# Last batch of a fused attention and expert kernel: q and k banked by token range, x in halves, last stores over two queues

## The chip, the cores and the metric

The kernel runs on one core of a Trainium2 chip. The metric is the device time of one execution in microseconds (us); the time of the kernel before is the median of six executions. Work is spread over TensorE (PE, with its weight loads as PEld), VectorE (DVE), ScalarE (ACT), GpSimd (POOL) and SyncE (SP), which here only issues DMA transfers. Each engine takes its instructions in the order in which the kernel writes them.

## The reference

Two layers follow one another. The first is attention over 8 batches, 12 heads, 448 tokens and head size 64, with a soft cap on the scores:

```python
scores = cap * np.tanh(scale * (q @ k.T) / cap)
attn = softmax(scores)          # over the keys
x[b] = concat_heads(attn @ v)   # 448 x 768
```

The second takes `x` through four single-head causal attention experts and adds those of the two best gate values per token:

```python
w = softmax(top2(x @ w_gate))
for e in range(4):
    q, k, v = x @ wq[e], x @ wk[e], x @ wv[e]
    ye = softmax(causal(scale * q @ k.T)) @ v @ wo[e]
    out += (token picked e) * w * ye
```

## The kernel before, in words

**Body.** The first layer runs over 48 pairs of heads, six pairs per batch. For each pair PE fills score banks (`fill`, L459), ACT takes `tanh` out of them (`tanh`, L478, instruction at L483) and then one `exp` over the whole pair (`expo`, L488, instruction at L491). PE multiplies with v (`blk`, L509), DVE normalises (L528, L532), PE transposes the result and one copy puts it into `xT[b][:, j, :]` (`a_xt_tr`, `a_xt_out`), the slice j of x for that batch. The second layer of batch b is done while the pairs of batch b+1 run. The order on ACT is a fixed list, `prog`. What PE and DVE do between the fills is chosen by `Plan`, which keeps estimated clocks for PE, DVE and ACT. `do_fill` (L945) sets `rel`, the time at which ACT gives a score bank back, `cost`, PE's time for the fill, and lets `plan.pump` place other work ahead of the fill as long as that ends before ACT is due, less `cost` and a margin of 0.3.

**Tail.** The last batch (b = 7) has no following pairs to hide behind. `last_batch` (L1053) collects all that is left of batch 6 (called c), the last pairs' attention and the whole second layer of batch 7 as operations with estimated costs, engines, dependencies and PSUM banks; `Graph.solve` (L155) tries 4000 priority lists and keeps the order with the smallest estimated end. An operation that may run on either DVE or ACT (`both`, L1082) is given to the one that would end it first. Priorities are the length of the path to the end plus a hand-set bias (L1089 to L1099): operations of the first token half (A, tokens below `CUT` = 256) get +6, the output projections (`wo`) and stores of batch c get -`BW` = -4.

For batch 7 the tail holds, in the order of the data: pv of the last pair in two halves of tokens (`("pv", u, i)`); four transposes into one bank and one copy of 448 columns to `xT` (`("xtp", u)`, `("xt", u)`); q and k of two expert pairs r = 0, 1 in four banks of 448 columns each (`qk_mm`, L1045, six matmuls per bank, L670), each evacuated by one copy of 448 columns (`q_out`, `k_out`); gate logits in the spare columns of the bank of q, r = 1 (`logits`, L1183); v (`v_mm`, L1194); scores in banks A, B and C (`fill`, L1259; A is tokens below 256, B and C the rest), their `exp` (L1293), pv (`pv_mm`, L1320), normalisation and gate weight (L1340 to L1357), transposes (`ot_tr`, L1359), projection (`project`, L1152, matmuls at L809), copies to the output tile `ob` (`b_wo_out`, L817) and stores (`b_store`, L826, on the SP queue). A store waits for both column halves of its `ob` tile, except for the last window (n = 3, 64 rows), which is stored in two halves. Some of the q and k matmuls of the last batch (`EARLY`, L1051) are given to `Plan` and run before the tail.

Of the kernel before, what the change touches and what calls it, by code (L numbers as in the profile page):

```python
# [132 lines left out]
class Graph:  # L133
# [55 lines left out]
    def order(self, users, deps, count, prio, eps):  # L189
        n = len(self.ops)  # L190
        free = dict(self.free)
        left = [len(d) for d in deps]
        start_at = [o[6] for o in self.ops]
        pools = {k: list(v) for k, v in self.pools.items()}
        slot = dict(self.held)
        count = dict(count)
        ends = {}
        ready = [i for i in range(n) if not left[i]]
        out = []
        span = 0.0  # L200
        while ready:
            cand = []
            for i in ready:
                _, eng, _, _, groups, opens, _, _ = self.ops[i]
                t = start_at[i]
                pool = None
                if opens:
                    m = len(groups)
                    ts = [
                        (max(f for _, f in pools[k][0:m]), k) for k in opens if len(pools[k]) >= m  # L210
                    ]
                    if not ts:
                        continue
                    f, pool = min(ts)
                    t = max(t, f)
                e = min(eng, key=lambda e: max(t, free[e]) + eng[e])
                cand.append((max(t, free[e]), i, e, pool))
            if not cand:
                return None
            first = min(c[0] for c in cand)  # L220
            t, i, e, pool = max((c for c in cand if c[0] <= first + eps), key=lambda c: prio[c[1]])
            _, eng, _, _, groups, opens, _, _ = self.ops[i]
            end = t + eng[e]
            free[e] = end
            span = max(span, end + self.LAND * (e == "DMA"))
            ready.remove(i)
            out.append((t, len(out), i, e, pool))
            for g in groups:
                if opens:
                    slot[g] = pool  # L230
                    pools[pool].pop(0)
                ends[g] = max(ends.get(g, (t, 0.0)), (t, end + self.LAT[e]))
                count[g] -= 1
                if not count[g]:
                    insort(pools[slot[g]], ends[g])
            for u in users[i]:
# [9 lines left out]
def kernel(  # L246
# [576 lines left out]
        ps = s.pop(("wo", n, f))  # L823
        evac(ob[lo:128, f * (D // 2) : (f + 1) * (D // 2)], ps[lo:128, :], act)

    def b_store(b, n, fs=(0, 1)):  # L826
        lo = 64 if n == 3 else 0
        w = WIN[n]
        c = slice(fs[0] * (D // 2), (fs[-1] + 1) * (D // 2))
        nc.sync.dma_start(out[b, w + lo : w + 128, c], st[b]["ob", n][lo:128, c])  # L830

    def b_wo(b, n, f):
        b_wo_ps(b, n, f)
# [111 lines left out]
    def do_fill():  # L945
        nonlocal nfill
        o = reads[nfill]
        rel = ends[nfill - 2] if nfill >= 2 else 0.0
        cost = 0.42 if o[0] == "X" or o[2] else 0.19
        for d in fill_dep(o):  # L950
            plan.force(d)
        cost = plan.pe_time(cost, plan.pe)
        at = plan.act + sum(dur(x) for x in prog[pos : where[nfill]])
        plan.pump(rel, at - cost - 0.3)
        plan.pe = max(plan.pe, rel, *(plan.done[d] for d in fill_dep(o))) + cost
        fill(*o[1:]) if o[0] == "T" else b_fill(*o[1:])
        plan.done[("f", nfill)] = plan.pe + plan.LAT
        nfill += 1
# [10 lines left out]
    def slot(p):  # L969
# [25 lines left out]
        if p >= HP and p % HP == 0 and p < NP:  # L995
            batch(p // HP - 1)
        if p == NP - 2:
            for r, w in EARLY:
                for j in range(4):
                    g = ("qk", r, w)  # L1000
                    d = [("xt", NP - HP + j)] + [(*g, j - 1)] * (j > 0)
                    plan.add(
                        (*g, j), 0.19, 0.0, d, nom["E", NP - 1, 0] + j, qk_mm, r, w, j,
                        aux="open" if j == 0 else None, group=g,
                    )

# [33 lines left out]
    BANKS["C", 0] = [(r, k, max(k, KM * (k == TAIL)), S) for r in range(2) for k in (TAIL, 256)], 64  # L1040


    qk = {}

    def qk_mm(r, w, j):  # L1045
        if j == 0:
            qk[r, w] = bank([128, 512], f32, f"{w}ps_{B - 1}_{r}")
        b_qk_mm(B - 1, r, w, qk[r, w][:, 0:S], j, j + 1)


    EARLY = ((0, "q"), (0, "k"))  # L1051

    def last_batch():  # L1053

# [20 lines left out]
            dict(aux=[(0.0, t) for t in plan.aux], tail=[(0.0, t3)] * 4),  # L1075
        )

        BR, BA, BW, BX = 2.0, 6.0, 4.0, 4.0

        BOTH = ("aux", "tail")  # L1080

# [3 lines left out]
        def op(key, eng, deps, fn, *args, group=None, groups=(), opens=None):  # L1085
# [2 lines left out]
            f = (lambda e: fn(*args, e == "ACT")) if len(eng) > 1 else (lambda e: fn(*args))  # L1088
            bias = 0.0  # L1089
            if key[0] == "qk":  # L1090
                bias = BR * (key[1] == 0)
# [8 lines left out]
            G.op(key, eng, deps, f, groups, opens, after, bias)  # L1100


        for u in (p - 1, p):
            for i in range(2):
# [10 lines left out]
                op((*g, "rc"), {"DVE": 0.18}, [(*g, 1, 1)], a_pv_rc, u, i, group=g)  # L1115
                op((*g, "xk"), {"DVE": 0.43}, [(*g, "rc")], a_pv_xk, u, i, group=g)
            g = ("xtp", u)
            for i in range(2):
# [45 lines left out]
            op((*g, 2), both(0.57, 0.49), [(*g, rs[-1])], b_wo_out, b, n, f, group=g)  # L1164

        def store(b, n):
            for fs in ((0,), (1,)) if (b, n) == (B - 1, 3) else ((0, 1),):
                kb = max(0.62, 0.5 * len(fs) * (0.5 if n == 3 else 1.0))
                op(
                    ("st", b, n, fs), {"DMA": kb}, [("wo", b, n, f, 2) for f in fs], b_store, b, n,  # L1170
                    fs,
                )

        for n in range(4):
# [5 lines left out]
                store(c, n)  # L1180


        def logits(j):  # L1183
            for n in range(4):
                nc.tensor.matmul(
                    qk[1, "q"][:, S + E * n : S + E * (n + 1)],
                    xT[b][:, j, WIN[n] : WIN[n] + 128], wvg[:, j, E * Dh : E * Dh + E],
                    start=False, stop=(j == NDC - 1), skip_group_check=True,
                )
# [17 lines left out]

        def lg_out():
            nc.vector.tensor_copy(
                s["lg"], qk[1, "q"][:, S : S + 4 * E].rearrange("p (n e) -> p n e", e=E)  # L1210
            )

        def q_out(r, act=False):
            b_q_out(b, r, qk[r, "q"][:, 0:S], act)

        def k_out(r, act=False):
            b_k_out(b, r, qk[r, "k"][:, 0:S], act)

        x0 = p - NDC + 1
        for r in range(2):  # L1220
            for w in "qk":
                g = ("qk", r, w)
                for j in range(NDC):
                    if (*g, j) in plan.done:
                        G.held[g] = "aux"
                        continue
                    d = [("xt", x0 + j)] + [(*g, j - 1)] * (j > 0)
                    op(
                        (*g, j), {"PE": 0.19}, d, qk_mm, r, w, j, group=g,
                        opens=None if j else BOTH,  # L1230
                    )
                d = [(*g, NDC - 1)] + [("el", NDC - 1)] * (r == 1 and w == "q")
                op((*g, "out"), both(0.6, 0.53), d, q_out if w == "q" else k_out, r, group=g)
        g = ("qk", 1, "q")
        for j in range(NDC):
            d = [("xt", x0 + j), (*g, 0)] + [("el", j - 1)] * (j > 0)
# [4 lines left out]
        for m in range(2):  # L1241
            g = ("vl", m)
            prev = None
            for j0, j1 in ((0, 3), (3, 5), (5, 6)):
                for i in range(2):
                    d = [("xt", x0 + j1 - 1), prev or ("xtp", p, 0)]
# [9 lines left out]

        sl = {}

        def fill(x):  # L1259
            blocks, _ = BANKS[x]  # L1260
            for e in range(2):
# [2 lines left out]
            for i, (r, k0, q0, q1) in enumerate(blocks):  # L1264
                for e in range(2):
                    h = slice(64 * e, 64 * (e + 1))
                    nc.tensor.matmul(
                        sl[x, e][:, o : o + q1 - q0], s["ke", r][h, k0 : k0 + 128],
                        s["qe", r][h, q0:q1], start=(i == 0),
                        stop=(i == len(blocks) - 1 and x[0] == "B"), skip_group_check=True,  # L1270
                    )
                o += q1 - q0
# [24 lines left out]
        for x, (blocks, o0) in BANKS.items():  # L1297
            rs = {a[0] for a in blocks}
            for e in range(2):
# [8 lines left out]
            g = [("sL", x, e) for e in range(2)]  # L1308
            op(
                ("sL", x, "mm"), {"PE": dict(A=0.6, B=0.25, C=0.8)[x[0]]},  # L1310
                [("qk", r, w, "out") for r in rs for w in "qk"], fill, x, groups=g, opens=BOTH,
            )
            for e in range(2):
                op(
# [166 lines left out]
```

## Time and profile before

| What | Value |
|---|---|
| Median of 6 executions | 326.96 us (326.5 to 327.65) |
| The profiled execution, its own time | 326.9 us |
| Span of its instructions | 325.2 us |
| ACT busy | 307.2 us, 94% of the span |
| PE busy | 277.6 us, 85% |
| DVE busy | 215.0 us, 66% |
| POOL busy | 155.7 us, 48% |
| Mean granted TensorE clock | 0.981 |

Times below are microseconds from the first instruction of the profiled execution. In the views of the profile a row names the line of the kernel, the engine, the operation, what it writes and reads, the shape and how often it ran; a bracket at the end says how long the engine had been idle and what released it. A row of a table by stretches gives the busy time of each engine in the stretch. The time of an execution is 1.7 us more than its span (326.9 against 325.2); a change of the span is taken to be a change of the time.

### The profile page before, as it was taken

To read this page: it belongs to the slowest core of one execution; us is meant where nothing else is said; L and a number is where in the kernel's file an instruction comes from. 1 tells how busy PE (TensorE), PEld (TensorE's weight loads), DVE (VectorE), ACT (ScalarE), POOL (GpSimd) and SP (SyncE) were. 2 spreads that over 40 slices of the span, in tenths; PEclk is the share of its full clock that TensorE was granted. 3 is DMA by queue.
4 is the path that set the end of the run, shared out by engine and by line. 5 is a ranking of instruction groups with operands and counts; after the bars stand their busy time and mean duration, and the time that the engine had idled before them with its cause. 6 is when DMAs were issued, how large, how long until landed. Compare 5 with 4: busy or idle time off the path is not lost.

```text
span 325.2 us, 8853 instructions
## 1 busy us (share of the span) xinstructions
PE 277.6 (85%) x3335; PEld 177.9 (55%) x3335; DVE 215.0 (66%) x745; ACT 307.2 (94%) x306; POOL 155.7 (48%) x476
## 2 busy tenths in 40 slices
PE   6696788987899789998799889998789888988993
PEld 2264455645565556656556655556545565545761
DVE  4344545667677777678856886678846796567572
ACT  3989899999999999999999999999999999999583
POOL 3648999756806289865905385174713200202000
PEclk9999769999999999999999999999999999999998
DMA  7699999990173998879091991296002112020018
GB/s 153 180 226 247 213 229 242 210 202 2 54 215 103 264 248 236 223 174 194 0 254 66 233 262 44 97 237 178 3 1 99 48 26 100 2 74 2 2 63 278
DMA packets 65259, 46.20 MB, mean 142 GB/s; under 512 B 25984, under 2 KB 61696, under 8 KB 65216
## 3 DMA queue, kind: packets, MB, share of 16 engines
q1 hardware_dynamic: 54144, 43.58, 52.5%
q0 software_dynamic: 10512, 1.58, 7.4%
q8 instruction: 26, 0.43, 0.6%
q10 hardware_dynamic: 560, 0.48, 0.5%
q14 instruction: 17, 0.14, 0.1%
HBM read 36.19 MB, written 11.01 MB: 145 GB/s over the span
## 4 chain that ended last, share of the span: by engine, by line
ACT 72%; PE 8%; DMA 6%; issue 5%; POOL 4%; SPq 3%; DVE 1%; POOLq 0%
ACT y L483 34%; ACT p L491 29%; ACT pBs L727 9%; SPq L318 2%; DMA ktf<-in_k_dram 2%; DMA vtf<-in_v_dram 2%; PE wops L809 1%; DMA vf<-in_v_dram 1%; SPq L314 1%; DMA qf<-in_q_dram 1%; PE kps L670 1%; PE vps L589 1%; PE pv L519 1%; POOL q L391 1%; PE qps L670 1%
## 5 line engine op out<-in xcount | busy, mean ns | idle before, releaser
L483 ACT ACTIVATE y<-s 128x448 f16<-128x448 f32 x192 | 152.7, 960 | 3.2 <-PE s L463 1.9
L491 ACT ACTIVATE p<-y 128x3136 f16<-128x3136 f16 (+2 forms) x49 | 141.8, 2898 | 0.1
L735 POOL TENSOR_SCALAR_AFFINE_SELECT pBs<-pBs 128x128 f16<-128x128 f16 (+1 forms) x112 | 27.9, 279 | 115.5 <-ACT pBs L727 114.4
L467 PE MATMUL s<-qt,kt 64*128 64x448 f16 x288 | 52.4, 374 | 12.0 <-ACT y L483 9.9
L519 PE MATMUL pv<-v16s,p 128*128 128x65 f16 x1152 | 61.6, 197 | 0.0
L519 PEld LDWEIGHTS <-p 128*128 128x128 f16 x1152 | 53.3, 100 | 3.8 <-issue 0.7
L513 PE MATMUL pv<-vtzs,p 128*128 128x130 f16 x192 | 43.6, 228 | 12.5 <-ACT p L491 11.3
L532 DVE TENSOR_TENSOR xk<-pv,rc 128x256 f16<-128x256 f32 x96 | 40.7, 424 | 3.3
L528 DVE RECIPROCAL rc<-pv 128x4 f32<-128x4 f32 x96 | 17.3, 180 | 38.3 <-PE pv L519 37.2
L467 PEld LDWEIGHTS <-kt 64*128 64x128 f16 x288 | 18.8, 94 | 31.5 <-issue 21.9
L513 PEld LDWEIGHTS <-p 128*128 128x128 f16 x192 | 18.9, 99 | 31.1 <-ACT p L491 18.7
L376 DVE COPY ob<-wops 128x384 f32<-128x384 f32 (+1 forms) x52 | 28.7, 554 | 10.7 <-PE wops L809 10.1
L727 ACT ACTIVATE pBs<-sB 128x960 f16<-128x960 f32 (+1 forms) x28 | 31.3, 1118 | 0.0
L391 POOL CAST q<-qf 112x512 f16<-112x512 f32 x46 | 28.2, 613 | 5.9 <-DMA qf<-in_q_dram 4.0
L809 PE MATMUL wops<-wo,oT 128*128 128x384 f16 x128 | 29.6, 327 | 0.1
L589 PE MATMUL vps<-wvg,xT 128*128 128x260 f16 (+1 forms) x192 | 29.0, 275 | 0.0
L405 POOL CAST v16s<-vf 128x384 f16<-128x384 f32 x48 | 24.4, 508 | 5.9 <-DMA vf<-in_v_dram 3.1
L392 POOL CAST k<-kf 128x384 f16<-128x384 f32 x48 | 24.4, 508 | 4.2 <-DMA kf<-in_k_dram 4.2
L410 POOL CAST vtzs<-vtf 64x64 f16<-64x64 f32 x96 | 22.7, 237 | 3.7 <-DMA vtf<-in_v_dram 0.9
L670 PE MATMUL qps<-xT,wq 128*128 128x448 f16 x96 | 24.2, 352 | 0.0
L437 DVE COPY qt<-tps 128x384 f16<-128x384 f16 x48 | 16.9, 352 | 10.4 <-PE tps L427 10.2
L376 DVE COPY xT<-xtp 128x448 f16<-128x448 f16 x47 | 18.1, 385 | 8.5 <-PE xtp L554 8.3
(121 smaller groups left out, 453.8 us busy)
## 6 DMA issues: line engine op xcount, KB each, us to landing
qf<-in_q_dram SPq DMA_DIRECT2D x22, 448.0 KB, 6.4
out_dram<-ob SPq DMA_DIRECT2D x24, 384.0 KB, 2.8
kf<-in_k_dram SPq DMA_DIRECT2D x22, 384.0 KB, 6.9
vf<-in_v_dram SPq DMA_DIRECT2D x22, 384.0 KB, 6.4
ktf<-in_k_dram SPq DMA_DIRECT2D x44, 32.0 KB, 6.1
vtf<-in_v_dram SPq DMA_DIRECT2D x44, 32.0 KB, 5.5
out_dram<-ob SPq DMA_DIRECT2D x7, 192.0 KB, 3.0
kf<-in_k_dram SPq DMA_DIRECT2D x4, 192.0 KB, 3.5
```

What stands on the lines that cost most here:

```text
L376: (nc.scalar.copy if act else nc.vector.tensor_copy)(dst, src)
L391: eng.tensor_copy(q16, qf.rearrange("p h (c d) -> p c h d", c=QC))
L467: nc.tensor.matmul(sc[:, g, 0:S], kt[r, 128 * i : 128 * (i + 1)], qt[r, :], start=True, stop=True,)
L483: nc.scalar.activation(y[(p, g)][:, o : o + n, :], score.pop((p, i))[:, 0:n, 0:S], AF.Tanh, scale=isc / capf,)
L491: nc.scalar.activation(pt[:, 0:n, :], y.pop((p, g))[:, 0:n, :], AF.Exp, scale=capf)
L513: nc.tensor.matmul(pv[:, n, :, :], pt[:, o, w : w + 128], vtz[p % 12], start=(n == 0), stop=False, skip_group_check=True,)
L519: nc.tensor.matmul(pv[:, n, g, :], pt[:, o + g, w : w + 128], v16[p % 12][:, g, j - 1, :], start=False, stop=(j == KC), skip_group_check=True,
L532: nc.vector.tensor_tensor(xt[p][:, 2 * i : 2 * i + 2, :, :], pv[:, :, :, 0:Dh], rc.broadcast_to((128, 2, 2, Dh)), ALU.mult,)
L589: nc.tensor.matmul(ps, xT[b][:, j, w : w + 128], wvg[:, j, 0 : ps.shape[1]], start=(j == 0 and first), stop=(j == NDC - 1), skip_group_che ...
L670: nc.tensor.matmul(ps, w2[r][:, j, :], xT[b][:, j, :], start=(j == 0), stop=(j == NDC - 1), skip_group_check=(b == B - 1),)
L727: nc.scalar.activation(pb[:, o0 : o0 + n], st[b].pop(("sc", r, g))[:, 0:n], AF.Exp, scale=isc)
L809: nc.tensor.matmul(ps, st[b]["oT", r][:, w : w + 128], wo2[r][:, f * (D // 2) : (f + 1) * (D // 2)], start=(r == 0), stop=(r == 1),)
```

## The change

Five edits, all of them in what is planned or run at the end, save the second, which concerns every fill:

- `Graph.order` adds the landing time of 2.8 to the operations named `st` instead of to those on the engine DMA. With the new choice of engine for stores this is the same set of operations.
- `do_fill` takes ACT's release of a bank 0.15 later, the cost of a two-head fill as 0.36 instead of 0.42, and the margin as 0.25 instead of 0.3.
- q and k of batch 7 are held by tokens: bank ("A", r) has q and k of pair r for tokens 0 to 255, bank ("B", r) those for tokens 256 to 447, with the logits behind them in ("B", 1). Each step j is two matmuls of 256 or 192 columns in place of one of 448 per bank; each bank is evacuated in one copy of 512 or 384 columns. The scores of A need only the A banks, those of C only the B banks. The early groups are now ("A", 0) and ("A", 1).
- x of the last pair is transposed into two banks, one per half, and copied in two halves; the A matmuls of the last step wait for the A half alone.
- The stores of windows 2 and 3 of batch 7 are each done in two column halves, and each half may go on the SP or on the ACT queue. The estimate for a DMA store is at least 0.5 (0.62 before), and 0.5 of ACT's time for one on ACT. `BW` goes from 4.0 to -5.0, so the projections and stores of batch c get +5 where they had -4.

The diff, cut to its core:

```diff
-            span = max(span, end + self.LAND * (e == "DMA"))
+            span = max(span, end + self.LAND * (self.ops[i][0][0] == "st"))
...
-    def b_store(b, n, fs=(0, 1)):
+    def b_store(b, n, fs=(0, 1), act=False):
...
-        nc.sync.dma_start(out[b, w + lo : w + 128, c], st[b]["ob", n][lo:128, c])
+        (nc.scalar if act else nc.sync).dma_start(out[b, w + lo : w + 128, c], st[b]["ob", n][lo:128, c])
...
-        rel = ends[nfill - 2] if nfill >= 2 else 0.0
-        cost = 0.42 if o[0] == "X" or o[2] else 0.19
+        rel = ends[nfill - 2] + 0.15 if nfill >= 2 else 0.0
+        cost = 0.36 if o[0] == "X" or o[2] else 0.19
...
-        plan.pump(rel, at - cost - 0.3)
+        plan.pump(rel, at - cost - 0.25)
...
-    def qk_mm(r, w, j):
+    TOK = {"A": (0, CUT), "B": (CUT, S)}
+
+    def qk_mm(h, r, j):
         if j == 0:
-            qk[r, w] = bank([128, 512], f32, f"{w}ps_{B - 1}_{r}")
-        b_qk_mm(B - 1, r, w, qk[r, w][:, 0:S], j, j + 1)
-
-
-    EARLY = ((0, "q"), (0, "k"))
+            qk[h, r] = bank([128, 512], f32, f"qk{h}_{r}")
+        x = xT[B - 1][:, j, slice(*TOK[h])]
+        n = x.shape[1]
+        for i, w in enumerate((wq2[r], wk2[r])):
+            nc.tensor.matmul(
+                qk[h, r][:, n * i : n * (i + 1)], w[:, j, :], x, start=(j == 0 and i == 0),
+                stop=(j == NDC - 1), skip_group_check=True,
+            )
+
+
+    EARLY = (("A", 0), ("A", 1))
...
-        BR, BA, BW, BX = 2.0, 6.0, 4.0, 4.0
+        BR, BA, BW, BX = 2.0, 6.0, -5.0, 4.0
...
+        def xt_tr(i):
+            xps[i] = bank([128, 256], f16, f"xtp_{p}_{i}")
...
+        def xt_out(i, act=False):
+            x = slice(*TOK["AB"[i]])
+            evac(xT[b][:, NDC - 1, x], xps[i][:, 0 : x.stop - x.start], act)
...
+            for i in range(2) if u == p else ():
+                op((*g, i), {"PE": 0.12}, [("pv", u, i, "xk")], xt_tr, i, group=(*g, i), opens=BOTH)
+                op(("xt", u, i), both(0.27, 0.3), [(*g, i)], xt_out, i, group=(*g, i))
...
-            for fs in ((0,), (1,)) if (b, n) == (B - 1, 3) else ((0, 1),):
-                kb = max(0.62, 0.5 * len(fs) * (0.5 if n == 3 else 1.0))
+            last = b == B - 1 and n > 1
+            for fs in ((0,), (1,)) if last else ((0, 1),):
+                kb = max(0.5, 0.5 * len(fs) * (0.5 if n == 3 else 1.0))
                 op(
-                    ("st", b, n, fs), {"DMA": kb}, [("wo", b, n, f, 2) for f in fs], b_store, b, n,
-                    fs,
+                    ("st", b, n, fs), {"DMA": kb, "ACT": 0.5} if last else {"DMA": kb},
+                    [("wo", b, n, f, 2) for f in fs], b_store, b, n, fs,
                 )
...
-        def k_out(r, act=False):
-            b_k_out(b, r, qk[r, "k"][:, 0:S], act)
+        def qk_out(h, r, act=False):
+            n = TOK[h][1] - TOK[h][0]
+            s["qk", h, r] = bp.tile([128, 2, n], f16, name=f"qk{h}_{b}_{r}", tag=f"qk{h}")
+            evac(s["qk", h, r], qk[h, r][:, 0 : 2 * n].rearrange("p (w n) -> p w n", w=2), act)
...
+        def part_of(w, r, h, x0, x1):
+
+            half = "A" if x1 <= CUT else "B"
+            o = TOK[half][0]
+            return s["qk", half, r][h, w, x0 - o : x1 - o]
...
-                [("qk", r, w, "out") for r in rs for w in "qk"], fill, x, groups=g, opens=BOTH,
+                [("qk", h, r, "out") for r in rs for h in dict(A="A", B="AB", C="B")[x[0]]], fill, x, groups=g, opens=BOTH,
```

More of the change, by code (lines that the diff above doesn't have):

```diff
@@ L997, in slot @@
         if p == NP - 2:
-            for r, w in EARLY:
+            for h, r in EARLY:
                 for j in range(4):
-                    g = ("qk", r, w)
+                    g = ("qk", h, r)
                     d = [("xt", NP - HP + j)] + [(*g, j - 1)] * (j > 0)
                     plan.add(
-                        (*g, j), 0.19, 0.0, d, nom["E", NP - 1, 0] + j, qk_mm, r, w, j,
+                        (*g, j), 0.21, 0.0, d, nom["E", NP - 1, 0] + j, qk_mm, h, r, j,
                         aux="open" if j == 0 else None, group=g,
@@ L1090, in op @@
             if key[0] == "qk":
-                bias = BR * (key[1] == 0)
+                bias = BR * (key[1] == "A")
             elif key[0] in ("pvL", "otL"):
@@ L1100, in op @@
             G.op(key, eng, deps, f, groups, opens, after, bias)
+        xps = {}
+        def xt_tr(i):
+            xps[i] = bank([128, 256], f16, f"xtp_{p}_{i}")
+            for n in (2 * i, 2 * i + 1):
+                nc.tensor.transpose(
+                    xps[i][:, 128 * (n - 2 * i) : 128 * (n - 2 * i + 1)],
+                    xt[p][:, n, :, :].rearrange("p g d -> p (g d)"), perm if n < 3 else pswap,
+                )
+        def xt_out(i, act=False):
+            x = slice(*TOK["AB"[i]])
+            evac(xT[b][:, NDC - 1, x], xps[i][:, 0 : x.stop - x.start], act)
         for u in (p - 1, p):
@@ L1117, in last_batch @@
             g = ("xtp", u)
+            for i in range(2) if u == p else ():
+                op((*g, i), {"PE": 0.12}, [("pv", u, i, "xk")], xt_tr, i, group=(*g, i), opens=BOTH)
+                op(("xt", u, i), both(0.27, 0.3), [(*g, i)], xt_out, i, group=(*g, i))
+            if u == p:
+                continue
             for i in range(2):
@@ L1180, in last_batch @@
                 store(c, n)
+        LG = 2 * (S - CUT)
         def logits(j):
@@ L1185, in logits @@
                 nc.tensor.matmul(
-                    qk[1, "q"][:, S + E * n : S + E * (n + 1)],
+                    qk["B", 1][:, LG + E * n : LG + E * (n + 1)],
                     xT[b][:, j, WIN[n] : WIN[n] + 128], wvg[:, j, E * Dh : E * Dh + E],
@@ L1209, in lg_out, with x_of @@
             nc.vector.tensor_copy(
-                s["lg"], qk[1, "q"][:, S : S + 4 * E].rearrange("p (n e) -> p n e", e=E)
+                s["lg"], qk["B", 1][:, LG : LG + 4 * E].rearrange("p (n e) -> p n e", e=E)
             )
-        def q_out(r, act=False):
-            b_q_out(b, r, qk[r, "q"][:, 0:S], act)
-        def k_out(r, act=False):
-            b_k_out(b, r, qk[r, "k"][:, 0:S], act)
+        def qk_out(h, r, act=False):
+            n = TOK[h][1] - TOK[h][0]
+            s["qk", h, r] = bp.tile([128, 2, n], f16, name=f"qk{h}_{b}_{r}", tag=f"qk{h}")
+            evac(s["qk", h, r], qk[h, r][:, 0 : 2 * n].rearrange("p (w n) -> p w n", w=2), act)
         x0 = p - NDC + 1
-        for r in range(2):
-            for w in "qk":
-                g = ("qk", r, w)
+        def x_of(j, half):
+            return ("xt", p, half) if j == NDC - 1 else ("xt", x0 + j)
+        for half, h in enumerate("AB"):
+            n = TOK[h][1] - TOK[h][0]
+            for r in range(2):
+                g = ("qk", h, r)
                 for j in range(NDC):
@@ L1226, in last_batch @@
                         continue
-                    d = [("xt", x0 + j)] + [(*g, j - 1)] * (j > 0)
+                    d = [x_of(j, half)] + [(*g, j - 1)] * (j > 0)
                     op(
-                        (*g, j), {"PE": 0.19}, d, qk_mm, r, w, j, group=g,
+                        (*g, j), {"PE": 0.00084 * n}, d, qk_mm, h, r, j, group=g,
                         opens=None if j else BOTH,
                     )
-                d = [(*g, NDC - 1)] + [("el", NDC - 1)] * (r == 1 and w == "q")
-                op((*g, "out"), both(0.6, 0.53), d, q_out if w == "q" else k_out, r, group=g)
-        g = ("qk", 1, "q")
+                d = [(*g, NDC - 1)] + [("el", NDC - 1)] * (r == 1 and h == "B")
+                op(
+                    (*g, "out"), both(0.17 + 0.0019 * n, 0.12 + 0.0018 * n), d, qk_out, h, r,
+                    group=g,
+                )
+        g = ("qk", "B", 1)
         for j in range(NDC):
-            d = [("xt", x0 + j), (*g, 0)] + [("el", j - 1)] * (j > 0)
+            d = [x_of(j, 1), (*g, 0)] + [("el", j - 1)] * (j > 0)
+            d += [x_of(j, 0)] * (j == NDC - 1)
             op(("el", j), {"PE": 0.1}, d, logits, j, group=g)
@@ L1245, in last_batch @@
                 for i in range(2):
-                    d = [("xt", x0 + j1 - 1), prev or ("xtp", p, 0)]
+                    d = [x_of(j1 - 1, m), prev or ("xtp", p, 0)]
                     prev = (*g, i, j0)
@@ L1267, in fill @@
                     nc.tensor.matmul(
-                        sl[x, e][:, o : o + q1 - q0], s["ke", r][h, k0 : k0 + 128],
-                        s["qe", r][h, q0:q1], start=(i == 0),
+                        sl[x, e][:, o : o + q1 - q0], part_of(1, r, h, k0, k0 + 128),
+                        part_of(0, r, h, q0, q1), start=(i == 0),
                         stop=(i == len(blocks) - 1 and x[0] == "B"), skip_group_check=True,
```

## The prediction, made before the changed kernel ran

> **What bounds the kernel now.** I read the page first, then busy time by stretches, the chain that ended last, and the SP queue's waits. The page shows ACT nearly always at work, and a dip at the end.
>
> ```profile
> PE 277.6 (85%) x3335; PEld 177.9 (55%) x3335; DVE 215.0 (66%) x745; ACT 307.2 (94%) x306; POOL 155.7 (48%) x476
> ...
> ACT  3989899999999999999999999999999999999583
> ```
>
> By stretches (columns: span, then busy time of PE, PEld, DVE, ACT, POOL, clock, DMA share, GB/s):
>
> ```profile
> 48.00:303.70 255.70, 225.90 (x2819) 146.85 (x2817) 181.84 (x619) 255.66 (x241) 122.44 (x396) 1.00 0.53 131
> ...
> 290.00:300.00 10.00, 8.62 (x128) 5.74 (x129) 6.57 (x27) 9.97 (x12) 2.26 (x10) 1.00 0.01 2
> 300.00:306.00 6.00, 6.00 (x109) 4.58 (x106) 3.64 (x14) 3.71 (x4) 0.00 (x0) 1.00 0.01 3
> 306.00:312.00 6.00, 6.00 (x74) 4.30 (x72) 3.54 (x13) 3.87 (x10) 0.00 (x0) 1.00 0.00 0
> 312.00:318.00 6.00, 6.00 (x80) 4.14 (x76) 4.73 (x23) 5.80 (x15) 0.00 (x0) 1.00 0.39 149
> 318.00:325.00 7.00, 1.67 (x10) 0.70 (x8) 1.42 (x4) 1.65 (x4) 0.00 (x0) 0.88 0.82 269
> ```
>
> From 48 to 303.70 ACT is idle for 0.04 us: nothing there can get shorter, and any late fill costs its whole lateness. From 300 to 318 PE is the full engine, while ACT has holes until 312. After 318 the DMA engines are what is busy. So three bounds follow each other: ACT, PE, stores. The chain near the end:
>
> ```profile
> 316.02 1.79 PE wops L809 x11
> 317.81 0.13 PE otLB L1363 x2
> 317.93 0.02 issue
> 317.95 0.27 DVE oT L376
> 318.22 0.05 issue
> 318.27 1.00 PE wops L809 x5
> 319.27 0.02 issue
> 319.29 1.04 DVE ob L376 x2
> ```
>
> PE stops for 0.34 (317.93 to 318.27), the only gap since 299.36; then come the last projections and two copies to `ob`, the second ending at 320.34 (319.78 + 0.56). Then the stores. Two answers of the timeline, each of one instruction of SP:
>
> ```profile
> 320.44 0.90 SPq L830 DMA_DIRECT2D out_dram<-ob  x1
> ```
>
> ```profile
> 321.44 0.54 SPq L830 DMA_DIRECT2D out_dram<-ob  x1
> ```
>
> The first is the 384 KB store of window 2, issued 0.10 after its second half was copied. It held SP for 0.90, and the last 96 KB half of window 3, whose copy on ACT had ended at 319.93, went out only at 321.44. It landed 2.77 later, at 324.21; 0.96 of closing semaphores makes 325.17.
>
> **The change part by part.**
>
> *q and k by tokens.* Removed: 24 matmuls of 448 columns, 0.19 each in the chain. Added: 24 of 256 columns and 24 of 192. The v matmuls (L589, 256 columns) go 11 in 1.20, or 0.109. Of 192 columns the trace has none over all rows: between 128 columns (two transposes of L554 in 0.11, 0.055) and 256 (0.109) the straight line gives 0.082, the value I take since 192 lies midway. Sum: 24 x 0.109 + 24 x 0.082 - 24 x 0.19 = +0.02; the ends give -0.6 and +0.7. The 24 more weight loads (0.10 each) lie beside the matmul before, as those of v do; uncovered they would cost up to 2.4. I take 0.
>
> Evacuation: four copies of 448 columns (0.53 on ACT, 0.62 on DVE) become two of 512 and two of 384. DVE takes 0.69 for 512 columns (`vall`) and 0.56 for 384 (`ob`); ACT between 0.38 (256 columns) and 0.70 (the 512-column exp). Engine time is about equal: 0.
>
> What moves is the start of the A scores. Now: the one copy of x ends at 306.99, the last copy of k at 309.20, the scores start at 309.40 and their first exp at 310.16. After: the first half of `xk` ends at 305.18; 0.34 to the transposes and 0.28 for them gives 305.80; a copy of 256 columns is 0.29 (`otLA`); four q and k matmuls 0.44 plus 0.25 until the last is out, 306.8; the 512-column copies 0.69, 307.5; then 0.20 and 0.76 as now: first exp at 308.4, some 1.7 earlier. ACT is free for it: it waits 2.75, 0.86 and 0.69 between 303.7 and 309.6. The ten exps of 310.16 to 314.31 follow each other without a gap, so the last could move by up to the same.
>
> *x in halves.* Transposes as before (four); one copy of 0.53 becomes 0.29 and 0.25, on either engine. Extra engine time about 0.1, in the holes of ACT just named; with that cover gone, 0.1.
>
> These two do not shorten PE's work. From 299.36 PE is full, and its last matmul starts at 319.42 and is through 0.16 later; unless work is drawn ahead of 299.36, it can win only its 0.34. That is late next when the exp wait goes. I take -0.34; the ends are 0 and -0.34 -1.38 (the idle PE time of 290 to 300, 10.00 - 8.62).
>
> *Projections of batch c first (`BW`).* The same work, moved. Each is two matmuls of 0.16 and a copy of 0.39 (ACT, back to back) to 0.56 (DVE); their four stores move along on SP. Put into ACT's holes before the exps they cost nothing, and DMA, idle until 314.71, starts earlier. Put ahead of the last exp on ACT, each costs 0.39 there.
>
> *Stores in halves, two queues.* One store more: ten at the end instead of nine, of which up to four may go to ACT; on SP an issue takes 0.33 to 0.90. An issue on ACT is in the trace only at the start (0.33 to 0.55); I take 0.5, behind ACT's copies, where nothing but the last copy (0.47) waits. The last half is then issued about 0.10 after its copy instead of 1.10: -1.00. Ends: 0 (if the bytes are the limit) and -1.10. The bytes: 2.75 MB go out from 315.5 to 323.87, at about 0.4 MB per us when dense, so 6.9 us without a hole; the DMA view of 313 to 325 in 40 slices falls to 164 to 246 GB/s between 318.7 and 320.2, a hole that is filled only if earlier stores come. With c's stores even 0.5 earlier, 315.0 + 6.9 = 321.9 is before the last issue's landing.
>
> [...] The row above has 0.90 for one issue, not small against 2.77. If the saving were only the shortest issue in the trace, 0.33, the sum would be -0.67 and the time 326.3.
>
> *Fills.* `rel` + 0.15 + 0.36 ends a fill 0.09 later in the plan, and other work may end 0.11 nearer to ACT's need. In the trace most fills end 0.36 or more before ACT is free; two end 0.08 and 0.09 before, and there the exp came 0.13 late each. Between 0.20 and 0.36 nothing is lost. About nine of 191 fills after 48 end under 0.32 before: 0.11 less costs them at most 0.06 each, 0.5 in all. Before 48, ACT waited five times for scores, 3.0 together; a new order may add or take one (0.6). I take 0, ends -1.2 and +1.7.
>
> *Landing by name.* The same operations, 0.
>
> **Sum.** -0.34 - 1.00 + 0.02 = -1.3. In the profiled execution: 325.2 - 1.3 = 323.9 of span, 326.9 - 1.3 = 325.6 of time; the profiled time is 0.06 under the median 326.96, which gives 325.6 to 325.7. I say 325.6, its own range 325.0 to 326.3.
>
> **The rivals.**
>
> A. *PE starts on the tail sooner.* For it: 1.38 of idle PE time from 290 to 300, and early groups of 0.22 a step where 0.19 stood. Against: PE waits there for results (`ke`, `osc`, a bank). With 0.9 of it: 324.7.
>
> B. *The bound stays PE and bytes.* For it: no gap in 18 us; the extra half store; copies dense on ACT to 318.7. New gaps in PE eat the 0.34, and the DMA engines stay full after 320 (269 GB/s over the last seven us), so half a us or less is won: 326.6, within 0.2%.
>
> C. *Projections of c in the way of the exps (slower).* Place: ACT between the first and the last exp. Eight copies of 0.39 are 3.1; the exps have at most 1.7 to give. From five copies on, the last exp is later than 314.31. After it 9.9 us follow (314.31 to 324.21), of which SP's 1.0 and PE's 0.34 can go. With all eight ahead and the exps no earlier: +3.1 - 1.3 = +1.8; with half the head start used up about +1.0: 328.0. Against: the search counts ACT's time.
>
> D. *Fills come late before 48 (slower).* Three more waits of 0.75 (the longest row has 0.8) are +2.25, less 1.3: 327.9. It decides from two such waits on. Against: the margin moved by 0.11 only.
>
> That the change does nothing is excluded by the two queues, which the code issues if the search picks ACT; if it never does, B.
>
> **How the numbers follow.** Forecast 0.50 (325.6), A 0.15 (324.7), B 0.13 (326.6), C 0.13 (328.0), D 0.09 (327.9). A measurement of this kernel can tell about 0.2%, 0.65 us, from no change. Faster by more: forecast and A, 0.65. Within: B, 0.13. Slower: C and D, 0.22. The range reaches over A to 324.2 and up to D's 327.9; beyond lie most of C and the ends of A.
>
> **What would show it.** Right: the first exp of L1293's successor near 308.4; no PE gap after 299.4; c's first store before 314; the last two stores issued within 0.6 of each other on two queues; the last landing about 2.8 after the last copy. Wrong: waits of ACT for scores after 48, or more than 3.0 before; copies of `ob` between the exps; an SP or ACT issue near 0.9 ahead of the last half; DMA still dense to the end.

## The result, and the profile after

The changed kernel takes 325.18 us (median of 21 executions, 323.98 to 325.77). The kernel before, run beside it, takes 326.53 (median of 47). The ratio of the means is 0.9951 (95% interval 0.9939 to 0.9964), or 1.6 us less (2.0 to 1.2 less); the two medians differ by 1.35. The forecast of 325.6 was 0.4 off. Its number held, but by luck: most of its sum did not hold, as the experiments show.

The page of the changed kernel, busy time and the row of ACT:

```profile
PE 277.3 (86%) x3359; PEld 180.5 (56%) x3359; DVE 215.6 (67%) x746; ACT 307.7 (95%) x306; POOL 155.6 (48%) x476
...
ACT  3989999999999999999999999999999999999792
```

The same stretches at the end as before (busy time of PE, PEld, DVE, ACT, POOL, clock, DMA share, GB/s):

```profile
300.00:306.00 6.00, 6.00 (x103) 5.12 (x103) 3.10 (x11) 5.20 (x6) 0.00 (x0) 1.00 0.01 3
306.00:312.00 6.00, 6.00 (x79) 4.63 (x78) 3.81 (x15) 4.84 (x13) 0.00 (x0) 1.00 0.18 70
312.00:318.00 6.00, 5.60 (x76) 3.79 (x74) 4.58 (x18) 5.11 (x12) 0.00 (x0) 1.00 0.49 163
318.00:325.00 7.00, 0.83 (x6) 0.29 (x3) 1.02 (x2) 0.85 (x2) 0.00 (x0) 0.92 0.60 197
```

PE is done sooner (0.83 after 318 where it was 1.67), and 70 GB/s move already between 306 and 312, where the kernel before moved nothing. The first stores in the tail, of the changed kernel (four issues up to 316.5) and of the kernel before (two up to 316); such a row has the start of the first issue and the time to the end of the last:

```profile
305.54 10.52 SPq L830 DMA_DIRECT2D out_dram<-ob  x4
```

```profile
314.71 1.58 SPq L830 DMA_DIRECT2D out_dram<-ob  x2
```

The chain of the changed kernel at its end (the last row stands on the line that closes the program; the stores are not on this chain):

```profile
316.71 0.44 DVE oscLB L1398
317.15 0.05 issue
317.20 0.28 PE otLB L1407 x2
317.48 1.04 PE wops L809 x6
318.52 0.02 issue
318.55 0.56 DVE ob L376
319.11 0.46 DVEq L1520
```

And its last issues, two on each queue:

```profile
318.88 1.11 SPq L830 DMA_DIRECT2D out_dram<-ob  x2
319.14 1.01 ACTq L830 DMA_DIRECT2D out_dram<-ob  x2
```

The last copy ends at 319.57, the last issue starts 0.03 later, at 319.60, and the last landing is at 322.82. Before, these were 320.34, 321.44 and 324.21.

**Where the time went.** The end of the last pair's exp on ACT (L491) divides an execution into a body, in which ACT is nearly always busy (254.50 of 255.00 us from 48 to 303 in the changed kernel), and a tail. In the profiled executions the body ended at 303.71 before and at 304.32 after; the tail is the difference to the span. The answers for the two tails, before and after:

```profile
303.71:325.17 21.46, 15.96 (x201) 10.94 (x197) 11.05 (x42) 11.32 (x27) 0.00 (x0) 0.96 0.38 130
```

```profile
304.32:323.84 19.52, 14.12 (x182) 10.01 (x180) 10.27 (x39) 11.67 (x28) 0.00 (x0) 1.00 0.42 142
```

The tail is 1.94 shorter and has 1.84 less of PE's work in it; the body of this execution is 0.61 longer. So the question became why PE has less left to do, and whether that, or something else that came with it, ends the execution sooner.

### The profile page after: what moved, and what is told of

It is laid out like the page before. It is cut to its first block, busy times and chain, and to the rows that moved or that the text cites. A ratio compares the mean times of both kernels' runs of the same rounds, so it can differ in the third digit from the quotient of the medians.

```text
span 323.8 us, 8892 instructions
## 1 busy us (share of the span) xinstructions
PE 277.3 (86%) x3359; PEld 180.5 (56%) x3359; DVE 215.6 (67%) x746; ACT 307.7 (95%) x306; POOL 155.6 (48%) x476
## 4 chain that ended last, share of the span: by engine, by line
ACT 71%; PE 10%; DMA 8%; issue 6%; DVE 3%; POOL 1%; DVEq 0%; SPq 0%
ACT y L483 34%; ACT p L491 27%; ACT pBs L727 9%; DMA qf<-in_q_dram 3%; DMA kf<-in_k_dram 2%; DMA ktf<-in_k_dram 2%; PE pv L519 1%; PE s L467 1%; PE wops L809 1%; PE vps L589 1%; PE tps L420 1%; PE qkB L1053 1%; PE s L463 1%; PE tps L427 1%; PE pv L513 1%
## 5 line engine op out<-in xcount | busy, mean ns | idle before, releaser
L491 ACT ACTIVATE p<-y 128x3136 f16<-128x3136 f16 (+2 forms) x49 | 140.7, 2877 | 0.1
L519 PE MATMUL pv<-v16s,p 128*128 128x65 f16 x1152 | 63.4, 197 | 0.0
L519 PEld LDWEIGHTS <-p 128*128 128x128 f16 x1152 | 54.1, 100 | 5.3 <-issue 0.7
L513 PE MATMUL pv<-vtzs,p 128*128 128x130 f16 x192 | 43.8, 228 | 11.3 <-ACT p L491 10.1
L376 DVE COPY ob<-wops 128x384 f32<-128x384 f32 (+1 forms) x53 | 29.3, 554 | 10.2 <-PE wops L809 10.1
L467 PEld LDWEIGHTS <-kt 64*128 64x128 f16 x288 | 18.0, 94 | 31.8 <-issue 22.5
L513 PEld LDWEIGHTS <-p 128*128 128x128 f16 x192 | 19.0, 99 | 29.4 <-ACT p L491 17.9
L809 PE MATMUL wops<-wo,oT 128*128 128x384 f16 x128 | 30.5, 327 | 0.1
L589 PE MATMUL vps<-wvg,xT 128*128 128x260 f16 (+1 forms) x192 | 30.1, 275 | 0.0
L376 DVE COPY xT<-xtp 128x448 f16<-128x448 f16 (+2 forms) x49 | 18.7, 381 | 9.5 <-PE xtp L554 8.9
L397 POOL CAST ktzs<-ktf 64x64 f16<-64x64 f32 x92 | 21.4, 232 | 3.1 <-DMA ktf<-in_k_dram 0.3
```

Of the source, the lines that this page charges most:

```text
L376: (nc.scalar.copy if act else nc.vector.tensor_copy)(dst, src)
L467: nc.tensor.matmul(sc[:, g, 0:S], kt[r, 128 * i : 128 * (i + 1)], qt[r, :], start=True, stop=True,)
L491: nc.scalar.activation(pt[:, 0:n, :], y.pop((p, g))[:, 0:n, :], AF.Exp, scale=capf)
L513: nc.tensor.matmul(pv[:, n, :, :], pt[:, o, w : w + 128], vtz[p % 12], start=(n == 0), stop=False, skip_group_check=True,)
L519: nc.tensor.matmul(pv[:, n, g, :], pt[:, o + g, w : w + 128], v16[p % 12][:, g, j - 1, :], start=False, stop=(j == KC), skip_group_check=True,
L589: nc.tensor.matmul(ps, xT[b][:, j, w : w + 128], wvg[:, j, 0 : ps.shape[1]], start=(j == 0 and first), stop=(j == NDC - 1), skip_group_che ...
```

## The experiments

All kernels in one table. "Time" is the change against the kernel before as it ran in the same round of runs, from the ratio; rows of different rounds are compared only by way of it. The other columns come from one profiled execution each, in us after the end of the last pair's exp, apart from "body", the end of that exp itself.

| Kernel | Time, % (interval) | Body | First store | Last copy | Last landing | End |
|---|---|---|---|---|---|---|
| before | 0 | 303.7 | 11.0 | 16.6 | 20.5 | 21.5 |
| after (the change) | -0.5 (-0.6 to -0.4) | 304.3 | 1.2 | 15.3 | 18.5 | 19.5 |
| before_stores_two_queues | +0.2 (0.0 to +0.4) | 302.5 | 11.0 | 16.6 | 21.3 | 22.2 |
| after_stores_SP_only | -0.6 (-0.8 to -0.4) | 302.5 | 1.2 | 15.2 | 18.4 | 19.3 |
| after_BW_4 | -0.5 (-0.6 to -0.3) | 303.4 | 1.8 | 15.2 | 18.8 | 19.7 |
| before_split_only | 0.0 (-0.2 to +0.2) | 302.5 | 10.7 | 16.6 | 20.4 | 21.4 |
| before_fill_only | -0.3 (-0.5 to 0.0) | 304.1 | 2.6 | 15.6 | 19.7 | 20.6 |
| after_old_fill | -0.1 (-0.3 to +0.2) | 302.1 | 10.0 | 16.6 | 21.4 | 22.3 |
| before_cost_only | +0.6 (+0.3 to +0.8) | 306.4 | 8.8 | 15.8 | 19.8 | 20.7 |
| after_unsplit | -0.1 (-0.3 to +0.2) | 304.5 | 1.7 | 16.0 | 19.6 | 20.5 |
| before_half_of_v | -0.1 (-0.2 to +0.1) | 303.0 | 10.3 | 15.9 | 20.2 | 21.2 |
| after_other_search | -0.3 (-0.4 to -0.1) | 304.4 | 0.7 | 15.8 | 19.1 | 20.2 |
| after_unsplit_other_search | -0.4 (-0.6 to -0.2) | 302.9 | 1.8 | 15.2 | 19.2 | 20.2 |
| after_stores_of_6_late | +0.3 (+0.1 to +0.5) | 303.2 | 11.3 | 15.3 | 21.5 | 22.5 |

The theory I began with (theory 1) was that of the prediction: the last half of a store waited for SP, and the second queue takes that wait away. The rivals were early bytes, and luck.

**The queues alone.** Every matmul and copy stays where it was; only the last stores change. In the loop that emits the planned operations:

```diff
+            if key[0] == "st" and key[1] == b and key[2] > 1:
+                continue
             G.ops[i][3](e)
+            if key[0] == "wo" and key[1:3] == (b, 3) and key[4] == 2:
+                b_store(b, 3, (key[3],))
+        for f in range(2):
+            b_store(b, 2, (f,), True)
```

> The kernel before with its order on PE, DVE and every copy unchanged; only the last stores differ: window 2 in two halves on the ACT queue behind ACT's last copy, each half of window 3 on SP right behind its copy. Theory 1 (the last half waited 1.0 us for SP and that wait is most of the gain): the last issue starts near 320.4 instead of 321.44, the time falls by 0.6 to 1.0 us. Rival 2 (the gain is that projections and stores of the batch before came early, so that bytes and copies end sooner; the queue is only where they leave): the bytes are dense after 320, the last landing moves by 0.3 at most. Rival 3 (luck of the search, or the body): no change.

Measured: 1.0017 (0.9998 to 1.0035), no gain. The last issue did start sooner, 0.33 after the last copy instead of 1.10, and the last landing came later, 4.71 after the copy instead of 3.87. The DMA view of its end, issues with size and median time to landing:

```profile
out_dram<-ob SPq DMA_DIRECT2D x4, 384.0 KB, 3.3
out_dram<-ob ACTq DMA_DIRECT2D x2, 192.0 KB, 4.2
...
out_dram<-ob SPq DMA_DIRECT2D x2, 96.0 KB, 4.0
```

A half of 192 KB took 4.2 to land and one of 96 KB 4.0, where before the two stores of 96 KB took 3.1: what was saved up to the last issue (0.77) was more than spent between that issue and its landing (4.38 instead of 2.77), and the last landing came 0.84 later.

**The queue taken away again.** The changed kernel with `(nc.scalar if act else nc.sync).dma_start` put back to `nc.sync.dma_start`, all else in its place.

> The changed kernel with its order on PE, DVE and of every copy unchanged; the two halves that went on the ACT queue go on SP, in the order of the plan. Theory 1: four issues of 0.4 to 0.6 us follow each other on SP from 318.9 on, the last starts near 320.3 instead of 319.6, the time rises by 0.4 to 0.7 us over the changed kernel. Rival 2: no more than 0.2. Rival 3: 0.

Measured: 0.9939 (0.9917 to 0.9962), no slower than the change itself. Its last two issues on SP:

```profile
318.26 1.10 SPq L830 DMA_DIRECT2D out_dram<-ob  x2
```

The second starts at 318.83, or 16.32 after the exp, 1.04 later than in the changed kernel (15.28); yet the last landing is 18.39 after the exp against 18.50. Theory 1 has fallen on both sides: an earlier issue landed no earlier. With the second queue the last issue came 1.04 us sooner here, and the last landing 0.11 later.

**The bias.** `BW` back to 4.0 in the changed kernel.

> The changed kernel with the old bias for the projections and stores of batch 6 (BW 4.0); the search runs anew. Theory 1: their stores start late again, but the last issue still waits for nothing; the time rises by 0.3 us or less. Rival 2: their stores start after 313 and the bytes pile up at the end as before; the time rises by 0.7 us or more. Rival 3: any size, and no tie with when the stores start.

Measured: 0.9955 (0.9936 to 0.9974). The stores of batch 6 still start 1.8 after the exp. So the early stores are there, but the bias does not bring them.

**The split alone.** The changed kernel with old fill constants, old bias and old stores.

> q and k by tokens and x in halves alone: old fill constants, old bias, old stores on SP. Theory 1: the exps start 1 us earlier or so, PE stays full, the end moves by 0.3 us at most and the last half still waits for SP. Rival 2 in the form that the split is what moves the end: the time falls by 0.7 us or more. Rival 3: any size.

Measured: 1.0002 (0.9983 to 1.0021). The exps of the last batch start 5.40 after the last pair's exp instead of 6.45, as intended; the last copy and the end stay where they were.

That left the fill constants, which I had costed at nothing, so I formed three new theories: F, S and B.

**The fill constants alone, and without them.** First `rel`, `cost` and the margin of the change in the kernel before; then their old values in the changed kernel:

```diff
-        rel = ends[nfill - 2] + 0.15 if nfill >= 2 else 0.0
-        cost = 0.36 if o[0] == "X" or o[2] else 0.19
+        rel = ends[nfill - 2] if nfill >= 2 else 0.0
+        cost = 0.42 if o[0] == "X" or o[2] else 0.19
...
-        plan.pump(rel, at - cost - 0.25)
+        plan.pump(rel, at - cost - 0.3)
```

> The kernel before with the three new fill constants alone. In the program's order the matmuls behind the last fill add up to 17.64 us of columns, against 19.19 before and 17.42 in the changed kernel. Theory F (the new constants put some 1.6 us more of the second layer's PE work between the fills, and PE sets the end): from the last pair's exp to the end 20.0 or less instead of 21.46, the time falls by 1.0 to 1.7 us. Theory S (the parts need each other: less work on PE only shows where the exps and the early stores have moved too): 0.6 us or less. Theory B (the body of the profiled run was merely luckier in its clock): no change of the stretch after the last exp.

> The changed kernel with the old fill constants; 19.09 us of matmul columns behind the last fill. Theory F: the stretch after the last pair's exp goes back to 21 or more, the time is within 0.5 us of the kernel before. Theory S: half of the gain stays, 0.7 us. Theory B: the stretch stays near 19.5.

Measured: 0.9972 (0.9948 to 0.9996) with them alone, 0.9994 (0.9974 to 1.0015) for the change without them. Without them nothing of the gain is left; with them alone some 0.9 us of the 1.6. The tail of the first:

```profile
304.06:324.70 20.64, 14.91 (x193) 9.91 (x190) 10.90 (x38) 11.38 (x28) 0.00 (x0) 0.95 0.40 135
```

PE's work is down by 1.05 and the first store leaves 2.6 after the exp. In all eight tails with the new `cost`, save the one with delayed stores below, the end is 19.3 to 20.7 after the exp; in those with the old one 21.2 to 22.3.

**One constant.** `cost` alone in the kernel before.

> The kernel before with only the planned cost of a fill changed from 0.42 to 0.36; 17.42 us of columns behind the last fill. Theory F: as with all three constants, 1.0 to 1.7 us faster, unless fills now come late: then ACT waits for scores after 48, and what that costs is seen there. Theory S: 0.6 or less. Theory B: no change of the stretch.

Measured: 1.0055 (1.0026 to 1.0084), slower. The tail is short (20.7), the body is not. ACT's waits for PE after 48:

```profile
ACT pBs L727 <- PE sB L708: 1.3, 1, 1.3
ACT y L483 <- PE s L467: 0.9, 2, 0.5
```

So `cost` lets more work in between the fills, and the fills come late: 2.2 of waits, where the kernel before had none. Of these, the 1.3 (at 64.4) came at full clock. The other two (0.45 at 122.27 and 0.50 at 153.81) lie in spells in which the granted clock was half (120.09 to 123.50 and 150.81 to 154.22), so they are not put down to the planner alone. Which of the later `rel` and the smaller margin keeps the body of the change short was not tried. This was rival D of the prediction, after 48 instead of before.

**The split taken out.** The changed kernel with the q, k and x of before; here, as in every kernel whose operations differ, the search runs anew.

> The changed kernel with q and k back in four banks of 448 columns and x copied whole; new fill constants, bias and stores; 17.64 us of columns behind the last fill. Theory F: within 0.4 us of the changed kernel. Theory S: the exps start 1 us later, and 0.7 us or more of the gain is lost. Theory B: as the changed kernel.

Measured: 0.9992 (0.9968 to 1.0016): most of the gain lost, which seemed to speak for S. But the search itself had not been tested. So the changed kernel and this one were run with `random.Random(2)` in `Graph.solve`, and, to settle F, the kernel before with PE relieved and nothing else: it leaves out half of the v matmuls of the last batch (`b_v_mm` stops at j = 3).

> The changed kernel with another start of the random search in Graph.solve (2 in place of 1). Theory F and S: the tail differs by 0.4 us at most, the time is within 0.4 of the changed kernel. Theory L (the search found a lucky order): the stretch after the last exp is 20.3 or more, half or more of the gain is lost.

> The changed kernel without the token split of q, k and x, with the other start of the search. Theory S: again about 20.5 from the last exp to the end, 0.7 us or more behind the changed kernel with either start. Theory L: anywhere between 19.5 and 21.

> The kernel before, every engine's order unchanged, with half of the v matmuls of the last batch left out (12 of 24, 0.11 us each, 1.3 us of PE and nothing of any other engine), so that its v is only part of the sum. Theory F (PE's load in the tail sets the end): the stretch from the last pair's exp to the end falls from 21.4 to 20.4 or less, the time by 1.0 us or more. Theory S (with the old split the copies, exps and stores are as late as PE): it falls by 0.2 to 0.7.

Measured: 0.9974 (0.9959 to 0.9990), 0.9960 (0.9942 to 0.9979) and 0.9994 (0.9978 to 1.0011). With the other start, the kernel with the split ends 20.16 after the exp and the one without it 20.15: that the split gains anything is not shown. The start of the search is worth 0.3 to 0.6 in the tail, and some 0.7 us in time for the changed kernel, with intervals that overlap a little. F and S had allowed 0.4 in the tail and L had asked for a stretch of 20.3 or more: neither is met to the letter, but nearly half of the 1.6 hangs on the order that one start found. Theory F falls as it was put. The tail with half of v:

```profile
303.04:324.21 21.17, 14.77 (x189) 9.94 (x185) 11.06 (x42) 11.33 (x28) 0.00 (x0) 0.96 0.39 132
```

PE has 1.19 less to do, the last copy comes 0.75 sooner, and the last landing 0.3. PE is not what ends the kernel before. What differs from `before_fill_only`, with as little PE work left, is the first store: 10.3 after the exp, not 2.6.

**The stores of batch 6 held back.** The last experiment takes from the changed kernel only that. On SP, the store of batch 6's last window (ready 11.3 after the exp) goes ahead of the other three:

```diff
+            if key[0:2] == ("st", c) and key[2] < 3:
+                held.append((i, e))
+                continue
             G.ops[i][3](e)
+            if key[0:3] == ("st", c, 3):
+                for i, e in held:
+                    G.ops[i][3](e)
```

> The changed kernel, every copy and matmul in its order; only SP's order differs: the store of batch 6's last window, ready some 11.3 us after the last pair's exp, goes first, so that the other three stores of batch 6 leave behind it instead of from 1.2 us on (in the kernel before they start at 11.0). Theory W (the bytes at the end are the limit, and what the change won is that the stores of batch 6 had left before): the last copy stays near 15.3 after the exp, the last landing comes 1 us or more later than 18.5, the time rises by 0.8 us or more over the changed kernel. Theory F (PE and the copies are the limit, the stores follow): the landing moves by 0.4 or less.

Measured: 1.0030 (1.0008 to 1.0052), 2.6 us over the change and slower than before. The last copy is where it was (15.25 after the exp in both), the last landing 3.04 later. The DMA views from 313 to 325, busy tenths and GB/s in 40 slices and the packets, of the changed kernel, of this one, and of the kernel before:

```profile
DMA  0000099930006992199999999899998000000000
GB/s 0 0 20 10 31 399 379 420 133 0 0 0 164 205 236 51 72 389 410 379 420 389 379 272 174 179 353 307 200 333 312 21 0 0 0 0 0 0 0 0
DMA packets 976, 1.99 MB, mean 166 GB/s; under 512 B 136, under 2 KB 520, under 8 KB 976
```

```profile
DMA  0000000069995999999999999999999999831000
GB/s 0 0 0 0 0 0 0 0 143 205 174 133 184 420 399 389 379 430 410 400 389 399 410 405 384 384 384 425 394 410 353 364 272 200 169 87 51 31 0 0
DMA packets 1248, 2.75 MB, mean 229 GB/s; under 512 B 160, under 2 KB 544, under 8 KB 1248
```

```profile
DMA  0000001059974999999999958999997999960000
GB/s 0 0 0 0 0 0 55 0 215 379 389 277 174 399 399 430 369 420 379 236 246 174 184 164 338 399 399 410 399 369 287 323 343 399 410 266 0 0 0 0
DMA packets 1105, 2.77 MB, mean 231 GB/s; under 512 B 144, under 2 KB 272, under 8 KB 1104
```

The second and the third have no free slice from the stores' first byte (315.55 in both) to the last: 2.75 MB in 8.8 and 8.3 us, or 0.31 and 0.33 per us, though the last copy comes 1.4 sooner after the exp in the second than in the third. The first has holes; 1.99 MB were left to it at 313, and its last four stores land 2.4 to 3.2 after their issue. The bytes end the kernel before, and the change wins because two of batch 6's four stores are out before 313. That is theory W, and this run decides for it.

Two limits remain. Not all of the 3.04 need be the early stores: `before_stores_two_queues` and `after_old_fill`, which also store halves over two queues behind full DMA engines, land 0.84 and 0.86 after the kernel before, and no run holds the stores back on SP alone. And how early is early enough is not shown: the first store of `before_cost_only` leaves only 8.8 after the exp, yet its tail (20.7) is nearly as short as that of `before_fill_only` (20.6), whose first store leaves at 2.6.

## Why the prediction was right, step by step

- **The number.** 1.3 less was forecast, 1.6 (1.2 to 2.0) measured. That they agree is luck: the term of -1.00 was worth nothing, and what stood in its place was costed at 0.
- **Stores, -1.00: wrong.** The issue wait went as described (the last issue 0.03 after the last copy), and it was worth nothing: no gain when added alone, no loss when taken away. The step that failed is the choice between the ends "0 (if the bytes are the limit) and -1.10". I had the DMA row, saw a hole at 318.7 to 320.2 in its rate, and took that as room. The engines' busy tenths stood at 9 in four of the five slices there and at 5 in the last: they were hardly free. The 6.9 us for the bytes took the dense rate throughout; the kernel before needed 8.3. (The -0.67 given for a saving of 0.33 leaves out the +0.02.)
- **Fills, 0: wrong.** This is where most of the gain comes from (some 0.9 of the 1.6 with them alone, nothing clear of noise without them). I weighed only what a later fill may cost ACT and not what the 0.06 less per fill lets in: in the program's order the matmuls behind the last fill fall from 19.19 to 17.42 us, an estimate from their columns (43,476 and 39,352 in the two traces, where 256 take 0.109); after the last pair's exp PE is busy for 14.12 us instead of 15.96. What a later fill costs ACT was not seen in the change: its one wait after 48, of 0.5 at 227.39, lies in a spell of half clock, and `after_stores_SP_only`, with the same fills in the same order and no such spell after 48, waits for none.
- **PE, -0.34: mis-sized.** The last copy came 1.38 sooner after the exp. Rival A had the direction (PE starts on the tail sooner), and not the place: 290 to 300 is as full as before (8.61 of 10.00, against 8.62); the work went in earlier. Less work on PE alone gains little at the end: 1.19 less of it in `before_half_of_v` moved the last landing by 0.3.
- **Split, earlier exps and no gain at the end: right.** First exp forecast 4.7 after the last pair's exp, 4.89 measured (6.45 before). +0.02 for the matmuls holds: in the changed kernel those of 256 columns start 0.109 apart and those of 192 columns 0.083, as taken (0.109 and 0.082).
- **Batch 6 first: the effect right, its cause wrong.** Early stores matter most, but it is the three fill constants together that bring them (2.6 after the exp; with `cost` alone 8.8, without them 10.0); the bias does nothing measurable.
- **Rival B ("the bound stays PE and bytes"): half right.** The bytes were the bound; what moved it was named nowhere in the sum. C did not happen. D happened where `cost` stands alone.
- **The signs.** Of those named for being right, the first store before 314 and the last two issues on two queues (0.15 apart) came; PE did get gaps (busy 5.60 of 6 from 312 to 318), and the last landing was 3.25 after the last copy, not 2.8. Of those named for being wrong, three came: a wait of ACT after 48, copies of `ob` between the exps (at 313.15 and 313.97, with two exps still to start at 314.47), and DMA dense to the end.

Left open: what the store halves give in the kernel before on SP alone (not tried), and how the 0.7 us between `before_fill_only` and the change, whose intervals overlap, divide between the other parts and the order that the search found. `after_stores_SP_only` beats the kernel before as the change does (0.9939 and 0.9951, intervals overlapping); the second queue can be left out.

## What to carry to other kernels

Ask of the last transfers first whether the DMA engines are busy without a gap up to the last byte. Where they were, in the kernel before, an earlier issue gained nothing (1.0017) and 1.19 less of PE's work moved the last landing by 0.3; what counted was to send early the bytes that can be ready early. A constant in a planner that looks like fine tuning can move more work across a stage than the rewritten stage itself; count the work left behind the boundary before costing it at nothing. And where a search orders the work, run each variant with two starts before crediting a part with the difference.

## What the runs showed of the hardware

The granted clock fell while ACT was full (busy 5.00 of 5 us from 220 to 225). In the changed kernel's trace PE was busy 3.27 of these 5 us, and then the clock was half for 3.41 us (224.95 to 228.36):

```profile
220.00:225.00 5.00, 3.27 (x46) 2.20 (x45) 4.12 (x19) 5.00 (x5) 0.96 (x4) 1.00 1.13 278
225.00:230.00 5.00, 4.68 (x69) 3.52 (x69) 2.81 (x11) 4.50 (x5) 4.36 (x13) 0.66 0.50 126
```

ACT waited there for a fill whose matmul took 0.56 instead of 0.35:

```profile
227.39 0.54 ACT L483 ACTIVATE y<-s 128x448 f16<-128x448 f32 x1 [0.50 <-PE s L463]
```

That trace has four spells of half clock from 33 us to its last instruction, each of 3.41 us, starting at 33.80, 44.05, 71.35 and 224.95: the later ones start 10.2, 27.3 and 153.6 after the one before, which is 3, 8 and 45 times the length of a spell (3.413). Ahead of the last one, from 221.53 to 224.95, PE was busy for 1.74 of 3.42 us, and no gap was longer than 0.78. In `after_stores_SP_only` PE was busy for 2.64 and for 2.14 us in two stretches of that length over the same matmuls (218.56 to 221.98 and on to 225.39), and the clock stayed full. What made the clock fall is not shown by these runs.

The tail repeats far better than the body. With the same order of matmuls and copies, the last copy came 15.25, 15.24 and 15.25 after the last pair's exp in three kernels, while their bodies ended at 304.3, 302.5 and 303.2. Half-clock spells after 48 came at 71 and 225 us in the first, nowhere in the second and at 225 in the third. That the body holds most of the spread between executions is read from these three profiles; the 1.8 between their bodies is as much as lies between the fastest and the slowest of the changed kernel's 21 executions.
